# New engine orders and engine choices for a windowed-attention and channel-mix kernel, planned with another rule for the shared port

## The chip, the core and the metric

The kernel runs on one core of a Trainium2 chip. A core has five engines with a queue of instructions each: TensorE (PE in the profile, with PEld for its weight loads), VectorE (DVE), ScalarE (ACT), GpSimd (POOL) and SyncE (SP), which here only starts DMAs. Each engine takes its own queue strictly in order, and engines wait for one another through semaphores. The metric is the device time of one execution in microseconds, lower is better.

## The reference

Attention over a causal window of 128 keys plus four sink keys, for 4 batches, 8 heads, 768 positions and 64 dimensions a head; then a channel mix over the 512 columns that the eight heads make together.

```python
scores = scale * np.matmul(q, k.transpose(0, 1, 3, 2))
is_sink = pos[None, :] < int(n_sink)                       # n_sink = 4
in_window = (rel >= 0) & (rel < int(window))               # rel = query - key, window = 128
scores = np.where(is_sink | in_window, scores, -1000000000.0)
a = np.exp(scores - max); a = a / (sum(a) + 1e-09)
x = np.matmul(a, v)                                        # then (B, S, 512)
x_prev = x shifted by one position
xk = mu_k * x + (1.0 - mu_k) * x_prev
xr = mu_r * x + (1.0 - mu_r) * x_prev
k = np.maximum(xk @ w_k, 0.0)                              # 512 -> 1024
out = 1.0 / (1.0 + np.exp(-(xr @ w_r))) * (k * k @ w_v)
```

## The kernel before

The positions are cut into twelve units of 256, three for each batch. A unit goes through these steps.

- **Load** (SP; L462 to L486, weights L505): q, k and v in 32-bit into three buffers each (`qs`, `ks`, `vs`). The weights come through three more (`w`).
- **Cast** to bf16 (L689, L693 or L698 for q and k into `qb` and `kb`, half a unit at a time; L770 for v into `vb`; L650 to L656 for the weights). Each may stand on ScalarE, VectorE or GpSimd; w_v is not cast by GpSimd.
- **Transpose** of q and k, on TensorE (L733, L738) with a copy out of PSUM (L751, L756, on ScalarE or VectorE), or by a transposing DMA for the units in `KD` and `QD`, 5 and later (L715).
- **Attend**: scores for two pairs of heads (L845), exponentials on ScalarE (L917), multiplication with the mask on VectorE (L931, tile `e`), sinks (L814, L821, then L888 or L903, the full or the tiled form of the same product), values (L950), reciprocal (L964) and scaling (L967, tile `x`) on VectorE.
- **Mix**: `x` is transposed to `xt` (L991 with a copy at L1000, or a DMA, L1011), a difference `td` (L1027) and from it `xk` and `xr` (L1040), all on VectorE but the copy.
- **FFN**: `xk` times w_k (L1117), relu (L1127 on ScalarE or L1131 on VectorE, tile `rl`), square (L1139, VectorE), `xr` times w_r (L1148), tanh (L1154), the square times w_v (L1166), the gate's product `ob` (L1175, VectorE), and the store (L1182). The last 128 rows have their own form (L1087, L1097).

No loop sets the order of the work. The program first lists 1028 operations, numbered as they are listed. Each has an engine, a price, the data it reads and writes, and the buffers that it takes and holds. The table `CHOICE` gives the engine or the form of the operations that could stand in several. The table `ORDER` gives, for each engine, the list of its operations in the order in which it takes them. `Plan.schedule` walks the five lists together by the prices; since each list is fixed, what it settles is which free buffer an operation gets, how the engines' parts are interleaved as the program is written, and where early fillers go: matmuls on the tile `warm` (L1226, L1229, L1232) whose results nobody reads, put where the plan sees TensorE idle before 28.5 us.

The plan takes VectorE and GpSimd to share a port to the on-chip memory, and marks operations that need it with `port=True`: casts, products of two tiles of that memory and stores started by GpSimd, but not operations that read PSUM, such as `x`, reciprocals, relus and `ob`. While one engine holds the port the plan lets no marked operation of the other begin.

```python
if o["port"]:
    t = max(t, port.get("DVE" if engine == "POOL" else "POOL", 0.0))
```

The program itself holds nothing of this rule: no semaphore stands for the port.

Of the kernel before, what the change touches and what calls it, by code (L numbers as in the profile page):

```python
# [18 lines left out]
    80: "ACT", 81: "POOL", 82: "ACT", 83: "POOL", 84: "POOL", 85: "ACT", 86: "ACT",  # L19
    88: "ACT", 90: "DVE", 96: "POOL", 98: "DVE", 99: "DVE", 101: "DVE", 102: "ACT",  # L20
    103: "ACT", 129: "POOL", 132: "DVE", 135: "POOL", 141: "ACT", 144: "DVE", 151:
    "DVE", 160: "PE/full", 172: "PE/full", 183: "POOL", 186: "DVE", 189: "POOL",
    192: "POOL", 195: "ACT", 196: "DVE", 198: "DVE", 242: "PE/full", 265: "DVE",
    268: "DVE", 271: "POOL", 273: "DVE", 274: "POOL", 277: "DVE", 278: "ACT", 352:
    "POOL", 355: "POOL", 361: "DVE", 380: "DVE", 428: "POOL", 432: "POOL", 438:
    "ACT", 496: "PE/full", 511: "POOL", 516: "ACT", 517: "ACT", 587: "POOL", 591:
    "ACT", 592: "ACT", 628: "POOL", 661: "POOL", 663: "POOL", 665: "ACT", 666:
    "ACT", 675: "DVE", 736: "POOL", 741: "ACT", 785: "POOL", 810: "POOL", 815:
    "DVE", 855: "POOL", 888: "DVE", 889: "ACT", 929: "POOL", 945: "PE/full", 998:
    "DVE", 1002: "DVE", 1006: "DVE", 1010: "DVE", 1019: "POOL",  # L30
# [17 lines left out]
FETCH = (17500.0, 28500.0, 36900.0, 47800.0, 57300.0, 66500.0, 78000.0, 85500.0,  # L48
         96000.0, 104000.0, 113000.0, 126000.0, 135000.0, 147000.0, 161000.0)
# [45 lines left out]
    ),  # L95
    "DVE": (
# [25 lines left out]
    ),  # L122
    "ACT": (
# [1166 lines left out]
```

## Time and profile before

| | |
|---|---|
| median of three runs | 166.36 us (165.06, 166.36, 167.31) |
| span of the profiled execution | 163.8 us; the profile gives no other time for it |
| from the span to the median | 2.5 us |
| chain that ended last, by engine | PE 69%, DVE 11%, DMA 10%, SP's queue 5% |
| DMA | 24.12 MB read, 6.29 MB written |
| GpSimd waiting for `ob` before a store | 47.0 us in 5 waits |

The span runs from the first to the last instruction of one execution; the runs' times hold what lies around it too. A group of instructions is written as line, engine, operation, tiles out<-in, shapes, count, then busy us and the mean ns of one, then the idle time ahead of it and who ended it. VectorE's and ScalarE's instructions overlap a little: one starts before the one ahead of it has ended, so sums of durations are above the busy time.

### The profile page before, as it was taken

How to read it: one execution, taken by the hardware profiler on the slowest of the kernel's cores; microseconds unless marked ns; L12 is line 12 of the kernel's file. 1: busy time of each engine (PE TensorE's matmuls, PEld its weight loads, DVE VectorE, ACT ScalarE, POOL GpSimd, SP SyncE). 2: the span in 40 equal slices, each digit the busy share in tenths (PEclk: the TensorE clock that was granted, in tenths of full speed). 3: DMA queues.
4: the chain of work that ended last, by engine and by line, in shares of the span. 5: the costliest groups of instructions: out<-in, count | busy, mean ns of one | idle time of the engine just before them, and what ended most of it. 6: DMA issues, size and time to landing. Idle time of an engine off the chain costs nothing.

```text
span 163.8 us, 4680 instructions
## 1 busy us (share of the span) xinstructions
PE 154.4 (94%) x1845; PEld 100.8 (62%) x1845; DVE 148.4 (91%) x383; ACT 121.4 (74%) x198; POOL 32.7 (20%) x61
## 2 busy tenths in 40 slices
PE   7989779899999999999999999999999999999991
PEld 2446458675468558777656666855385756578450
DVE  2589999999999999999999999998898989999931
ACT  3779899999999998999996689882499694152020
POOL 6643543222731022111103001032000100101001
PEclk9999999999999999999999999999999999999998
DMA  4999999999999999999997998979999963251032
GB/s 138 250 334 275 400 346 205 362 397 338 200 289 238 265 233 225 196 179 189 276 233 174 254 196 218 242 188 119 239 162 201 268 79 98 57 203 64 0 144 112
DMA packets 78821, 35.16 MB, mean 215 GB/s; under 512 B 68744, under 2 KB 71056, under 8 KB 78800
## 3 DMA queue, kind: packets, MB, share of 16 engines
q1 hardware_dynamic: 78384, 33.56, 85.8%
q0 software_dynamic: 400, 1.31, 2.3%
q8 instruction: 14, 0.23, 0.6%
q14 instruction: 7, 0.06, 0.1%
q10 hardware_dynamic: 16, 0.00, 0.0%
HBM read 24.12 MB, written 6.29 MB: 186 GB/s over the span
## 4 chain that ended last, share of the span: by engine, by line
PE 69%; DVE 11%; DMA 10%; SPq 5%; issue 2%; ACT 1%; POOL 0%; DVEq 0%; POOLq 0%
PE bank L1117 22%; PE bank L1166 19%; PE bank L1148 9%; PE bank L950 6%; DMA ks<-in_k_dram 5%; PE sc L845 4%; DMA kt<-kb 4%; DVE e L931 3%; SPq L462 3%; PE bank L1232 3%; DVE xk L1040 2%; DVE x L967 2%; PE bank L903 1%; SPq L479 1%; PE bank L991 1%
## 5 line engine op out<-in xcount | busy, mean ns | idle before, releaser
L1117 PE MATMUL bank<-xk,wk_sb 128*128 128x256 bf16 x384 | 47.3, 273 | 0.7 <-ACT rl L1127 0.5
L917 ACT ACTIVATE e<-sc 128x1024 bf16<-128x1024 f32 (+1 forms) x48 | 44.4, 966 | 3.4 <-PE sc L845 3.3
L1166 PE MATMUL bank<-wv_h,kk 128*128 128x512 bf16 x184 | 44.9, 379 | 0.0
L1117 PEld LDWEIGHTS <-wk_sb 128*128 128x128 bf16 x384 | 36.2, 98 | 7.0 <-issue 0.9
L931 DVE TENSOR_TENSOR e<-e,mask 128x1024 bf16<-128x1024 bf16 (+1 forms) x48 | 31.7, 676 | 0.0
L1127 ACT ACTIVATE rl<-bank 128x512 bf16<-128x512 f32 x43 | 25.1, 606 | 8.1 <-PE bank L1117 7.9
L1154 ACT ACTIVATE th<-bank 128x512 f32<-128x512 f32 x24 | 14.3, 608 | 18.2 <-PE bank L1148 11.4
L1166 PEld LDWEIGHTS <-kk 128*128 128x128 bf16 x184 | 17.0, 98 | 16.4
L1148 PE MATMUL bank<-wr_sb,xr 128*128 128x512 bf16 x96 | 23.8, 379 | 0.0
L1040 DVE SCALAR_TENSOR_TENSOR xk<-td,mu_all,xt 128x256 bf16<-128x256 bf16 x48 | 23.2, 511 | 0.0
L1040 DVE SCALAR_TENSOR_TENSOR xr<-td,mu_all,xt 128x256 bf16<-128x256 bf16 x48 | 22.4, 477 | 0.0
L967 DVE TENSOR_TENSOR x<-bank,rec 128x256 bf16<-128x256 f32 x48 | 19.5, 418 | 0.5
L1139 DVE TENSOR_TENSOR kk<-rl 128x512 bf16<-128x512 bf16 x48 | 19.3, 416 | 0.3 <-ACT rl L1127 0.2
L1175 DVE SCALAR_TENSOR_TENSOR ob<-th,bank 128x512 f32<-128x512 f32 x23 | 15.6, 682 | 2.4 <-PE bank L1166 1.1
L950 PE MATMUL bank<-vb,e 128*128 128x65 bf16 x352 | 16.5, 194 | 0.3
L950 PEld LDWEIGHTS <-e 128*128 128x128 bf16 x352 | 13.8, 97 | 3.5 <-DVE e L931 0.7
L1148 PEld LDWEIGHTS <-xr 128*128 128x128 bf16 x96 | 9.0, 98 | 9.6
L845 PE MATMUL sc<-qt,kt 64*64 64x128 bf16 (+3 forms) x496 | 12.6, 226 | 0.4 <-DMA kt<-kb 0.3
L1182 POOL DMA_DIRECT2D out_dram<-ob x5 | 2.8, 570 | 47.0 <-DVE ob L1175 47.0
L845 PEld LDWEIGHTS <-kt 64*64 64x64 bf16 (+1 forms) x496 | 9.0, 106 | 4.1 <-issue 1.4
L1027 DVE TENSOR_TENSOR td<-xt 128x512 bf16<-128x512 bf16 x24 | 10.1, 433 | 0.1
L770 ACT CAST vb<-vs 128x512 bf16<-128x512 f32 x14 | 8.8, 636 | 0.2 <-DMA vs<-in_v_dram 0.2
(93 smaller groups left out, 157.7 us busy)
## 6 DMA issues: line engine op xcount, KB each, us to landing
vs<-in_v_dram SPq DMA_DIRECT2D x24, 256.0 KB, 5.5
out_dram<-ob SPq DMA_DIRECT2D x18, 256.0 KB, 3.4
ks<-in_k_dram SPq DMA_DIRECT2D x16, 256.0 KB, 4.6
qs<-in_q_dram SPq DMA_DIRECT2D x12, 256.0 KB, 4.7
qs<-in_q_dram SPq DMA_DIRECT2D x6, 512.0 KB, 7.5
ks<-in_k_dram SPq DMA_DIRECT2D x4, 512.0 KB, 9.6
w<-in_moe_w_k_dram SPq DMA_DIRECT2D x2, 1024.0 KB, 8.8
w<-in_moe_w_v_dram SPq DMA_DIRECT2D x2, 1024.0 KB, 11.3
```

The source lines that it names most:

```text
L845: nc.tensor.matmul(out=sc[keys, a, o0 + f0 - q0:o0 + f1 - q0], lhsT=lhs[rows, keys], rhs=qs[rows, f0:f1], start=u not in BIAS, stop=True, ...
L917: nc.scalar.activation(out=buf[ek][:, :, lo:], in_=buf[sck][:, :, lo:], func=AF.Exp, scale=scale)
L931: nc.vector.tensor_tensor(out=at, in0=at, in1=m, op=ALU.mult)
L950: nc.tensor.matmul(out=o[:, g, a, :], lhsT=e[:, a, e0:e0 + 128], rhs=rhs, start=(T == 0 and i == 0), stop=(i == len(blocks) - 1), skip_gro ...
L967: P.op("DVE", dve(256), lambda ok=ok, rk=rk, c=c: nc.vector.tensor_tensor(out=buf["x", u][:, :, 128 * c:128 * c + 128].rearrange("p g (a d ...
L1040: nc.vector.scalar_tensor_tensor(out=buf[key][:, c, :], in0=buf[tk][:, i, :], scalar=mu[w][:, c:c + 1], in1=xt[:, c, t0 - 1:t0 + 255], op0 ...
L1117: nc.tensor.matmul(out=ps[:, i, :], lhsT=wk_sb[:, c, 128 * f:128 * f + 128], rhs=xk[:, c, :], start=(c == 0), stop=(c == NC - 1), skip_gro ...
L1127: nc.scalar.activation(out=buf[rk], in_=buf[psk].rearrange("p (i t) -> p i t", i=2), func=AF.Relu)
L1139: P.op("DVE", dve(512, 0.52), lambda f2=f2, rk=rk: nc.vector.tensor_tensor(out=buf["kk", u][:, 2 * f2:2 * f2 + 2, :], in0=buf[rk], in1=buf ...
L1148: nc.tensor.matmul(out=buf[psk], lhsT=buf["xr", u][:, c, 128 * g:128 * g + 128], rhs=wr_sb[:, c, :], start=(c == 0), stop=(c == NC - 1))
L1166: nc.tensor.matmul(out=buf[psk], rhs=wv_h[:, f, :], lhsT=buf["kk", u][:, f, 128 * g:128 * g + 128], start=(f == 0), stop=(f == NF - 1))
L1175: P.op("DVE", dve(512), lambda psk=psk, tk=tk, bk=bk: nc.vector.scalar_tensor_tensor(out=buf[bk], in0=buf[tk], scalar=1.0, in1=buf[psk], o ...
```

## The change

One line of the rule changes. A cast on GpSimd now holds the port in the plan for its price less 165 ns, where it was 0.58 of its price; `FETCH`, the moments at which the plan expects a fetch of instructions to delay the DMAs, has other numbers; and both tables were made anew, `ORDER` for all five engines and `CHOICE` with more entries.

```diff
-    80: "ACT", 81: "POOL", 82: "ACT", 83: "POOL", 84: "POOL", 85: "ACT", 86: "ACT",
+    80: "DVE", 81: "POOL", 82: "POOL", 83: "ACT", 84: "ACT", 85: "POOL", 86: "ACT",
...
-FETCH = (17500.0, 28500.0, 36900.0, 47800.0, 57300.0, 66500.0, 78000.0, 85500.0,
-         96000.0, 104000.0, 113000.0, 126000.0, 135000.0, 147000.0, 161000.0)
+FETCH = (17200.0, 24600.0, 35000.0, 47000.0, 53500.0, 62300.0, 71300.0, 80800.0, 90700.0,
+         102000.0, 111300.0, 123300.0, 132500.0, 145000.0)
...
     "DVE": (
-        70, 90, 71, 99, 98, 101, 109, 114, 111, 112, 106, 79, 116, 117, 132, 125,
+        70, 71, 93, 90, 95, 96, 98, 132, 114, 109, 129, 134, 131, 125, 106, 120,
...
             if o["port"]:
-                port[o["engine"]] = t + (0.58 * cost if o["engine"] == "POOL" else cost)
+                port[o["engine"]] = t + (max(0.0, cost - 165.0) if o["engine"] == "POOL" else cost)
```

No operation is added or removed; only the fillers go from 16 to 19. What stands on another engine than before:

- Early casts (q and k of units 0 to 4, v of units 0 to 3, and the weights): GpSimd makes 16 instead of 14, three of them weights before and after. Later casts: 22 instead of 13.
- VectorE, units 0 to 4: it gives up six casts of q, k and v, three copies of `xt` and two copies of `qt` or `kt` out of PSUM; it takes three casts, four copies of `qt` or `kt`, two relus and a quarter of w_k.
- In all: ScalarE eight operations fewer, VectorE three fewer, GpSimd eleven casts more and five stores fewer, SP five stores more.

Of the pairs of sink products the full form goes from 5 to 4, the tiled one from 11 to 12.

In the changed file all lines of the kernel's body stand 21 further down (L719 is L698). In the rows below the number in a tile's name tells its buffers apart; the number after the underscore has no meaning.

**VectorE at the start.** Before, from its fifth instruction on:

```order
L557 MEMSET hmask_150 128x520
L698 CAST kb0_79<-ks0_67 128x4x2x64
L561 MEMSET ksink0_151 128x64
L561 MEMSET ksink1_152 128x64
L561 MEMSET vsink0_153 128x520
L561 MEMSET vsink1_154 128x520
```

Now, from the last two of the same memsets on:

```order
L588 MEMSET sc0_61 64x2x64
L588 MEMSET sc1_62 64x2x64
L719 CAST qb0_82<-qs0_70 128x4x2x64
L719 CAST kb0_79<-ks0_67 128x4x2x64
L777 COPY qt0_89<-bank0_63 128x512
L719 CAST kb0_79<-ks0_67 128x4x2x64
L777 COPY kt0_85<-bank3_66 128x512
L710 CAST qb1_83<-qs1_71 128x2x4x64
L952 TENSOR_TENSOR e0_93<-e0_93,mask0_147 128x2x384
L952 TENSOR_TENSOR e1_94<-e1_94,mask0_147 128x2x384
L710 CAST kb1_80<-ks1_68 128x2x4x64
L772 COPY qt1_90<-bank3_66 128x128x4
```

All twelve memsets stand ahead of the first cast, three casts of unit 0 follow, and the cast of unit 1's q stands ahead of the first masks.

**SP at the start.** The first loads before:

```order
L486 DMA ks0_67<-in_k_dram 128x4x128
L486 DMA qs0_70<-in_q_dram 128x4x128 x2
L486 DMA ks0_67<-in_k_dram 128x4x128
L462 DMA vs0_73<-in_v_dram 128x8x64 x2
L479 DMA ks1_68<-in_k_dram 128x2x512
L479 DMA qs1_71<-in_q_dram 128x2x512
```

and now:

```order
L507 DMA qs0_70<-in_q_dram 128x4x128
L507 DMA ks0_67<-in_k_dram 128x4x128
L507 DMA qs0_70<-in_q_dram 128x4x128
L507 DMA ks0_67<-in_k_dram 128x4x128
L500 DMA qs1_71<-in_q_dram 128x2x512
L500 DMA ks1_68<-in_k_dram 128x2x512
L483 DMA vs0_73<-in_v_dram 128x8x64 x2
```

q comes ahead of k, and unit 1's q and k have moved ahead of unit 0's v.

**GpSimd's early casts.** Before, after the constants:

```order
L698 CAST kb0_79<-ks0_67 128x4x2x64
L621 COPY vsink0_153<-hmask_150 128x8
L621 COPY vsink1_154<-hmask_150 128x8
L787 COPY ksink0_151<-kt0_85 64x4x4 x2
L689 CAST kb1_80<-ks1_68 128x2x4x64 x2
L689 CAST qb2_84<-qs2_72 128x2x4x64
L770 CAST vb1_136<-vs1_74 128x8x64
L689 CAST kb2_81<-ks2_69 128x2x4x64 x2
L656 CAST wk_sb_139<-w320_76 128x4x256
L656 CAST wk_sb_139<-w321_77 128x4x256
```

and now:

```order
L719 CAST qb0_82<-qs0_70 128x4x2x64
L594 AFFINE_SELECT mask_146<-ones_157 128x128 x2
L710 CAST kb1_80<-ks1_68 128x2x4x64
L791 CAST vb0_135<-vs0_73 128x8x64
L808 COPY ksink0_151<-kt0_85 64x4x4 x2
L710 CAST kb2_81<-ks2_69 128x2x4x64 x2
L710 CAST qb2_84<-qs2_72 128x2x4x64
L791 CAST vb1_136<-vs1_74 128x8x64
L710 CAST qb2_84<-qs2_72 128x2x4x64
L710 CAST kb0_79<-ks0_67 128x2x4x64
L677 CAST wk_sb_139<-w320_76 128x4x256
L791 CAST vb2_137<-vs2_75 128x8x64
```

GpSimd now casts v of units 0, 1 and 2 and both halves of q of unit 2; the first weight stands behind nine short casts where it stood behind seven, and one half of k of unit 1 is no longer here.

More of the change, by code (lines that the diff above doesn't have):

```diff
@@ L18 @@
 CHOICE = {
-    80: "ACT", 81: "POOL", 82: "ACT", 83: "POOL", 84: "POOL", 85: "ACT", 86: "ACT",
[L20 to L30, printed above, removed]
+    80: "DVE", 81: "POOL", 82: "POOL", 83: "ACT", 84: "ACT", 85: "POOL", 86: "ACT",
@@ new lines @@
+    87: "DVE", 88: "ACT", 89: "DVE", 90: "DVE", 92: "ACT", 93: "DVE", 95: "DVE", 96:
+    "DVE", 98: "DVE", 99: "POOL", 101: "ACT", 102: "POOL", 103: "ACT", 129: "DVE",
+    131: "DVE", 132: "DVE", 134: "DVE", 135: "POOL", 137: "ACT", 138: "ACT", 140:
+    "ACT", 141: "POOL", 142: "ACT", 144: "ACT", 151: "ACT", 160: "PE/tiles", 172:
+    "PE/full", 183: "POOL", 185: "ACT", 186: "POOL", 188: "ACT", 189: "POOL", 191:
+    "ACT", 192: "POOL", 194: "ACT", 195: "ACT", 196: "POOL", 198: "ACT", 205: "ACT",
@@ new lines @@
+    213: "ACT", 217: "DVE", 221: "ACT", 225: "ACT", 234: "SP", 238: "SP", 242:
+    "PE/full", 254: "PE/tiles", 265: "POOL", 267: "ACT", 268: "ACT", 270: "ACT",
+    271: "ACT", 273: "ACT", 274: "ACT", 276: "ACT", 277: "POOL", 278: "POOL", 283:
+    "ACT", 290: "ACT", 298: "ACT", 302: "DVE", 306: "ACT", 310: "ACT", 319: "SP",
+    323: "SP", 346: "POOL", 348: "DVE", 349: "ACT", 351: "ACT", 352: "ACT", 354:
+    "ACT", 355: "ACT", 357: "ACT", 358: "POOL", 359: "POOL", 361: "DVE", 368: "ACT",
+    376: "ACT", 380: "ACT", 384: "ACT", 388: "ACT", 397: "SP", 401: "SP", 405:
@@ new lines @@
+    "PE/tiles", 417: "PE/tiles", 428: "POOL", 429: "POOL", 431: "ACT", 432: "POOL",
+    434: "ACT", 436: "ACT", 437: "POOL", 438: "DVE", 440: "ACT", 447: "ACT", 455:
+    "ACT", 459: "ACT", 463: "ACT", 467: "ACT", 476: "SP", 480: "SP", 484:
+    "PE/tiles", 496: "PE/tiles", 507: "POOL", 508: "POOL", 510: "ACT", 511: "ACT",
+    513: "POOL", 515: "ACT", 516: "ACT", 517: "POOL", 522: "ACT", 529: "ACT", 537:
+    "ACT", 541: "ACT", 545: "ACT", 549: "ACT", 558: "SP", 562: "SP", 585: "ACT",
+    586: "ACT", 587: "ACT", 589: "ACT", 591: "POOL", 592: "ACT", 607: "ACT", 611:
@@ new lines @@
+    "ACT", 615: "ACT", 619: "ACT", 628: "SP", 632: "SP", 636: "PE/tiles", 648:
+    "PE/tiles", 659: "ACT", 660: "ACT", 661: "POOL", 663: "POOL", 665: "ACT", 666:
+    "ACT", 668: "ACT", 675: "ACT", 683: "ACT", 687: "ACT", 691: "ACT", 695: "ACT",
+    704: "SP", 708: "SP", 712: "PE/tiles", 724: "PE/tiles", 735: "ACT", 736: "POOL",
+    737: "ACT", 739: "POOL", 741: "POOL", 742: "POOL", 760: "ACT", 764: "ACT", 768:
+    "ACT", 772: "ACT", 781: "SP", 785: "SP", 808: "POOL", 809: "ACT", 810: "ACT",
@@ L31 @@
+    812: "DVE", 814: "POOL", 815: "ACT", 830: "ACT", 834: "ACT", 838: "ACT", 842:
+    "ACT", 851: "SP", 855: "SP", 859: "PE/tiles", 871: "PE/tiles", 882: "ACT", 883:
+    "POOL", 884: "ACT", 886: "DVE", 888: "POOL", 889: "POOL", 904: "ACT", 908:
+    "ACT", 912: "ACT", 916: "ACT", 925: "SP", 929: "SP", 933: "PE/full", 945:
+    "PE/full", 970: "ACT", 974: "ACT", 978: "ACT", 982: "ACT", 991: "SP", 995: "SP",
+    998: "DVE", 1002: "ACT", 1006: "DVE", 1010: "DVE", 1019: "SP",
 }
```

138 rows, old and new, of the table ORDER are left out of this document.

## Prediction

> **What bounds the kernel now.** I read the page's busy shares first, then the busy time by stage, then the waits at the start, then VectorE's groups of instructions early against late. The first two lines come from the page, the others from the view by stage (stretch in us; length, then for each engine its busy us and instructions; granted clock; DMA share; GB/s).
>
> ```profile
> span 163.8 us, 4680 instructions
> PE 154.4 (94%) x1845; PEld 100.8 (62%) x1845; DVE 148.4 (91%) x383; ACT 121.4 (74%) x198; POOL 32.7 (20%) x61
> ...
> core 0: us, PE busy (x) PEld busy (x) DVE busy (x) ACT busy (x) POOL busy (x), PEclk, DMA share, GB/s
> ...
> 10.00:45.00 35.00, 31.06 (x433) 20.94 (x434) 34.74 (x85) 32.81 (x52) 14.13 (x16) 1.00 1.05 321
> 45.00:110.00 65.00, 64.90 (x887) 45.04 (x887) 63.84 (x169) 58.44 (x100) 9.12 (x15) 1.00 1.03 225
> 110.00:145.00 35.00, 34.69 (x391) 21.64 (x390) 32.64 (x86) 20.23 (x32) 2.45 (x6) 1.00 0.85 159
> ```
>
> From 10 to 45 us VectorE is busy 34.74 of 35 us and TensorE only 31.06: VectorE sets the pace. From 45 us TensorE is busy 64.90 of 65 and then 34.69 of 35: it sets the pace, and VectorE is 1.16 and 2.36 us below full, 3.5 us together. The granted clock is 1.00 throughout. So the end is the moment at which enough matmul work stands ready, plus a fixed line of matmuls: a microsecond that VectorE gains before 45 us comes off the end, one that it gains later does not, and one that it loses later costs nothing until the 3.5 us are used up. The chain that ended last says the same (start, us, what): VectorE's operations early, matmuls late, with a piece between them that runs over a load.
>
> ```profile
> 12.42 0.42 DVE x L967
> ...
> 28.00 0.41 DVE xk L1040
> 28.52 1.87 SPq L479
> ...
> 35.36 8.95 DMA ks<-in_k_dram
> 44.43 0.62 POOL kb L693
> ...
> 142.92 3.49 PE bank L1117 x32
> ```
>
> **The sum.** It has four terms and is made on the span, 163.8 us. The three runs shown have a median of 166.36 us, 2.5 us above it; I carry a change of the span to the median one for one.
>
> *Term 1, the port.* The rows that bear on it, first VectorE's groups from 10 to 46 us, then the same groups from 46 us on (xcount | busy us, mean ns):
>
> ```profile
> L931 DVE TENSOR_TENSOR e<-e,mask 128x1024 bf16<-128x1024 bf16 x8 | 6.7, 857 | 0.0
> L1040 DVE SCALAR_TENSOR_TENSOR xk<-td,mu_all,xt 128x256 bf16<-128x256 bf16 x9 | 5.5, 625 | 0.0
> L967 DVE TENSOR_TENSOR x<-bank,rec 128x256 bf16<-128x256 f32 x12 | 4.8, 412 | 0.1
> ...
> L931 DVE TENSOR_TENSOR e<-e,mask 128x768 bf16<-128x768 bf16 x7 | 4.1, 608 | 0.0
> L1027 DVE TENSOR_TENSOR td<-xt 128x512 bf16<-128x512 bf16 x6 | 2.8, 470 | 0.0
> L689 DVE CAST qb<-qs 128x512 bf16<-128x512 f32 x3 | 1.7, 555 | 0.0
> ...
> L1040 DVE SCALAR_TENSOR_TENSOR xk<-td,mu_all,xt 128x256 bf16<-128x256 bf16 x39 | 17.7, 485 | 0.0
> L931 DVE TENSOR_TENSOR e<-e,mask 128x1024 bf16<-128x1024 bf16 x24 | 16.2, 684 | 0.0
> L1027 DVE TENSOR_TENSOR td<-xt 128x512 bf16<-128x512 bf16 x18 | 7.3, 421 | 0.1
> L931 DVE TENSOR_TENSOR e<-e,mask 128x768 bf16<-128x768 bf16 x9 | 4.8, 546 | 0.0
> ```
>
> The same instruction is longer early: 8 x (857-684) + 9 x (625-485) + 7 x (608-546) + 6 x (470-421) ns is 1.38 + 1.26 + 0.43 + 0.29, and the three casts, 0.14 us each above the 0.41 of the undisturbed one quoted below, add 0.4: **3.8 us** of VectorE's time. Where it goes is seen when one operation is laid beside GpSimd's cast (timelines: start, us):
>
> ```profile
> 15.94 0.62 POOL L770 CAST vb<-vs 128x512 bf16<-128x512 f32 x1 [1.02 <-DMA vs<-in_v_dram]
> 16.00 0.83 DVE L1040 SCALAR_TENSOR_TENSOR xk<-td,mu_all,xt 128x256 bf16<-128x256 bf16 x1
> 21.51 1.51 POOL L656 CAST wk_sb<-w 128x1024 bf16<-128x1024 f32 x1 [1.87 <-DMA w<-in_moe_w_k_dram]
> 22.05 1.52 DVE L931 TENSOR_TENSOR e<-e,mask 128x1024 bf16<-128x1024 bf16 x1
> 40.11 1.89 POOL L689 CAST qb<-qs 128x512 bf16<-128x512 f32 x1 [6.39 <-DMA qs<-in_q_dram]
> ```
>
> The xk of 16.00 ends at 16.83; less the 0.485 that it takes undisturbed it was let go at 16.35, and the cast ended at 16.56. The e of 22.05 ends at 23.57, so it was let go at 22.89; the cast ended at 23.02. The hold ends 0.13 to 0.21 us before the cast does, as the new table has it (0.165). The old table ended it after 0.58 of its price: for a cast priced 620 ns after 360 instead of 455, for one priced 1100 after 638 instead of 935. Of the early casts (q and k of units 0 to 4, v of units 0 to 3 and the weights) GpSimd makes 11 of the short and 3 of the long kind, so 11 x 0.095 + 3 x 0.297 = 1.9 us of hold lay where the old order believed the port free, half of the 3.8. The change gives GpSimd 13 short and 3 long casts there; two more, at 0.095 each as the least, take 0.2 back. I take **-1.7 us**. The ends: all 3.8 us go, or nothing does and two more casts at 3.8/14 = 0.27 us each add 0.5.
>
> The Trainium skill, "SBUF — State Buffer", section "Who interferes with whom", says that whichever of the two engines issues first keeps the shared ports for the whole instruction. This trace shows 0.13 to 0.21 us less than that; by the page the old table left the whole 3.8 us uncounted (11 x 0.26 + 3 x 0.46 is more than that) and the new one leaves 16 x 0.165 = 2.6, the term would be 2.6 - 3.8 = -1.2 and the sum 165.2.
>
> *Term 2, work that changes engines in units 0 to 4.* VectorE gives up six casts, three xt copies and two copies out of PSUM, and takes three casts, four copies out of PSUM, two relus and one w_k cast. Prices, from the timeline at the start and the groups over the whole run:
>
> ```profile
> 6.22 0.41 DVE L698 CAST qb<-qs 128x512 bf16<-128x512 f32 x1
> 8.57 0.69 DVE L756 COPY kt<-bank 128x512 bf16<-128x512 bf16 x1 [1.95 <-PE bank L738]
> 9.18 0.68 DVE L756 COPY qt<-bank 128x512 bf16<-128x512 bf16 x1
> ...
> L1131 DVE TENSOR_SCALAR rl<-bank 128x512 bf16<-128x512 f32 x5 | 3.3, 685 | 0.3 <-PE bank L1117 0.3
> L1000 DVE COPY xt<-bank 128x512 bf16<-128x512 bf16 x5 | 2.1, 413 | 0.0
> L654 DVE TENSOR_SCALAR wv_h<-w 128x1024 bf16<-128x1024 f32 x2 | 1.4, 684 | 0.0
> ```
>
> The copy of 9.18 starts 0.08 before the one of 8.57 ends, so an operation costs 0.08 less than its row: a cast 0.33, an xt copy 0.33, a copy out of PSUM 0.61, a relu or (by the nearest row, L654) a w_k cast 0.60. Given up: 6 x 0.33 + 3 x 0.33 + 2 x 0.61 = 4.2. Taken: 3 x 0.33 + 4 x 0.61 + 2 x 0.60 + 0.60 = 5.2. That is **+1.0 us**. The ends: 0, where ScalarE, busy 32.81 of the 35 us, was what VectorE's order really followed, and +2.5, where what is given up would have come after 45 us anyway.
>
> *Term 3, the first waits.*
>
> ```profile
> 3.82 0.56 DVE L698 CAST kb<-ks 128x512 bf16<-128x512 f32 x1 [1.98 <-DMA ks<-in_k_dram]
> 4.58 1.04 DVE L561 MEMSET vsink<- 128x520 bf16 x2
> 4.69 0.62 ACT L698 CAST qb<-qs 128x512 bf16<-128x512 f32 x1 [2.38 <-DMA qs<-in_q_dram]
> 7.47 0.61 POOL L698 CAST kb<-ks 128x512 bf16<-128x512 f32 x1 [1.52 <-DMA ks<-in_k_dram]
> ```
>
> VectorE waits 1.98 us for the first load and 1.95 at 8.57: 3.9 in all. Its memsets run from 4.34 to 6.29; the change puts them ahead of the first cast, into the first wait, where their 1.9 us just fit. VectorE is then there at 3.82 and takes a cast that ScalarE had. But the loads still land at 3.82, 4.69 and 7.47, and VectorE's third cast is now the one that waits for 7.47: I count 0.1 + 0.3 + 1.7 and, for the transposes ahead of its next copy, 0.6, or 2.7 us of waits instead of 3.9. The q and k of unit 1 are now fetched ahead of unit 0's v, and the cast of that q stands ahead of VectorE's first masks; I allow 0.2 for it. **-1.0 us**. The ends: -1.95, the memsets' whole time, and 0, all of it lost to the later loads.
>
> *Term 4, the rest, at nothing.* ScalarE loses eight instructions; it is not the bound after 45 us. GpSimd has nine more of the later casts (22 for 13): VectorE's 3.5 us below full cover them, and without that cover each costs up to 0.455 (second rival). Five stores go from GpSimd's queue to SP's, where the loads behind them wait until ob is made; three buffers of each input cover that, and uncovered a load is late by one such wait. The last store was SP's already. On TensorE one pair of sink products changes from four full matmuls to eight on quarters of the array, and three fillers are added where it waits anyway; without that wait the first would cost 8/88 of 3.5 us, 0.3, less the full ones' own, and a filler its 0.4 us:
>
> ```profile
> L903 PE MATMUL bank<-vsink,es 64*64 64x130 bf16 x88 | 3.5, 226 | 0.0
> ...
> L1229 PE MATMUL bank<-warm 128*128 128x512 bf16 x6 | 2.5, 422 | 0.0
> ```
>
> -1.7 + 1.0 - 1.0 = -1.7 us: span 162.1, median **164.7 us**.
>
> **The rivals.**
>
> First: *the stall goes nearly whole, and the memsets' time with it.* For it: VectorE has x operations, which read PSUM and are not lengthened early (412 ns, no more than an undisturbed cast's 0.41 us), to lay beside a cast. -3.8 + 1.0 - 1.95 = -4.8: 161.6 us. Against it: casts start when their loads land, which no order fixes.
>
> Second, on the other side: *GpSimd's late casts become VectorE's new bound.* There are 22 of them instead of 13, on a VectorE with 3.5 us to spare. At a hold of 0.455 each, all stalling, 22 x 0.455 - 3.5 = +6.5 us: 171.2. At the early price, 22 x 0.27 - 3.5 = +2.4: 167.1. It decides for slower by 2% from 0.39 us a cast, (169.7 - 164.7 + 3.5)/22. Against it: the 13 late ones of now leave e at 684 ns. The Trainium skill, "Perfetto Trace Analysis", section "Optimizing Scalar/DVE Operations", warns that moving work between these two engines may not help since they share a port; the early rows bear it out, the late ones do not yet.
>
> Third: *nothing of the port is won.* The order is fixed while loads land when they land, so casts meet VectorE's operations as often as before, or the piece of the chain from 28.5 to 44.4 us, over SP's queue and a load of 8.95 us, takes back what VectorE gains. +0.5 + 1.0 - 1.0 = +0.5: 166.9 us. The new rule in the code alone moves nothing, since the lists set the order.
>
> **How the numbers follow.** Two per cent, about what a measurement of this kernel can tell from no change, is 3.3 us: faster is below 163.0, slower above 169.7. The forecast, 163.2 to 166.0, has 0.43; the first rival 0.20, the second 0.12, of which 0.08 lies above 169.7; the third 0.25. Of the forecast 0.04 falls below 163.0. So faster 0.24, same 0.68, slower 0.08. The range runs from near the first rival's 161.6 to past the third's 166.9 and the second's 167.1: 161.8 to 167.6, about 0.18 left out.
>
> **What would show it.** Right: VectorE's e (1024) and xk of the first 45 us fall from 857 and 625 ns to about 770 and 550; its waits before 10 us sum to some 2.9 us; TensorE is full from about 43 us. Wrong: early e above 820 ns; late e well above 684 (second rival); TensorE waiting after 45 us for a GpSimd cast (40.11 shows one of 1.89 us where 0.61 is its own length) or a load behind a store on SP.

## The result: 170.6 us, slower by 2.65%

| | before | after |
|---|---|---|
| median of 6 runs | 166.62 us (165.06 to 167.31) | 170.62 us (170.15 to 171.6) |
| ratio | | 1.0265, 95% interval 1.021 to 1.0321 |
| span of the profiled execution | 163.8 us | 169.9 us (its time 171.6) |

The profiled execution of the changed kernel is the longest of its six; their spans go from 168.4 to 169.9 us. So the two profiles differ by 6.1 us where the medians differ by 4.0, and a difference of 1 us between two profiles proves nothing here. The ratio, 1.0265, makes the loss 4.4 us of 166.4; the sections below reckon with ratios.

First the page of the changed kernel (busy us and share of the span, then the chain that ended last by engine), then the view by stage with the columns of before:

```profile
span 169.9 us, 4681 instructions
PE 155.0 (91%) x1834; PEld 100.5 (59%) x1853; DVE 152.3 (90%) x380; ACT 118.0 (69%) x190; POOL 36.6 (22%) x67
...
PE 41%; DVE 34%; DMA 16%; issue 3%; SPq 3%; ACT 1%; DVEq 0%; ACTq 0%
```

```profile
10.00:45.00 35.00, 30.12 (x435) 20.43 (x435) 34.12 (x80) 32.13 (x52) 13.61 (x19) 1.00 1.03 314
45.00:110.00 65.00, 62.69 (x852) 42.01 (x861) 63.55 (x160) 55.33 (x91) 13.85 (x22) 1.00 1.08 205
110.00:145.00 35.00, 33.65 (x383) 21.43 (x386) 32.48 (x85) 20.64 (x33) 3.46 (x5) 1.00 0.89 177
```

TensorE's busy time is 0.6 us longer than before (155.0 and 154.4); the rest of the 6.1 us is time in which it has nothing to do. It was full after 45 us and is no longer: 62.69 of 65 us and 33.65 of 35, where it had 64.90 and 34.69. VectorE's share of the chain went from 11% to 34%. The granted clock is 1.00 in all three stretches, as before.

The same by coarser stages, before and then after (the same columns); length less TensorE's busy time is its idle time:

```profile
0.00:45.00 45.00, 39.56 (x470) 24.88 (x471) 39.70 (x105) 38.80 (x61) 20.02 (x40) 1.00 0.99 295
45.00:60.00 15.00, 14.90 (x217) 10.21 (x217) 14.73 (x40) 14.27 (x25) 2.65 (x5) 1.00 1.15 258
60.00:145.00 85.00, 84.69 (x1061) 56.48 (x1059) 81.75 (x215) 64.39 (x107) 8.92 (x15) 1.00 0.93 192
```

```profile
0.00:45.00 45.00, 37.44 (x469) 24.08 (x471) 39.59 (x101) 36.19 (x58) 19.29 (x41) 1.00 0.97 296
45.00:60.00 15.00, 13.58 (x177) 8.78 (x180) 14.62 (x34) 13.17 (x22) 4.67 (x6) 1.00 0.80 169
60.00:145.00 85.00, 82.76 (x1071) 54.66 (x1072) 81.40 (x211) 62.80 (x102) 12.63 (x20) 1.00 1.05 199
```

TensorE's idle time grows from 5.44 to 7.56 us up to 45 us (+2.12), from 0.10 to 1.42 up to 60 us (+1.32) and from 0.31 to 2.24 up to 145 us (+1.93). With the 0.6 us of busy time this is 5.97 of the 6.1.

VectorE's groups of 10 to 46 us, the first five of the changed kernel and the last two of the kernel before, for two groups that the prediction did not show (xcount, busy us, mean ns):

```profile
L1061 DVE SCALAR_TENSOR_TENSOR xk<-td,mu_all,xt 128x256 bf16<-128x256 bf16 x12 | 7.0, 600 | 0.0
L952 DVE TENSOR_TENSOR e<-e,mask 128x1024 bf16<-128x1024 bf16 x8 | 6.3, 791 | 0.0
L1061 DVE SCALAR_TENSOR_TENSOR xr<-td,mu_all,xt 128x256 bf16<-128x256 bf16 x9 | 5.1, 572 | 0.0
...
L1048 DVE TENSOR_TENSOR td<-xt 128x512 bf16<-128x512 bf16 x6 | 3.3, 542 | 0.5 <-ACT xt L1021 0.5
...
L675 DVE TENSOR_SCALAR wv_h<-w 128x1024 bf16<-128x1024 f32 x2 | 1.8, 895 | 0.0
```

```profile
L1040 DVE SCALAR_TENSOR_TENSOR xr<-td,mu_all,xt 128x256 bf16<-128x256 bf16 x9 | 4.3, 473 | 0.0
...
L654 DVE TENSOR_SCALAR wv_h<-w 128x1024 bf16<-128x1024 f32 x2 | 1.4, 684 | 0.0
```

The mean of e fell from 857 to 791 ns and that of xk from 625 to 600. But xr rose from 473 to 572, td from 470 to 542, and the two casts of w_v from 684 to 895. Above the late rows that the prediction used: 8 x (791-684) + 12 x (600-485) + 6 x (542-421) ns is 0.86 + 1.38 + 0.73; xr and w_v above their undisturbed rows of before are 9 x 0.099 + 2 x 0.211 = 0.89 + 0.42. Together 4.3 us, where the prediction's sum was 3.8: the stall did not shrink, it changed its victims. Counted instruction by instruction, each against the usual length of its form, VectorE is lengthened by 4.3 us in twelve places before 50 us and 0.26 after 60 us in the old profile, and by 5.4 us in fourteen places before 50 us and 2.6 in nine after 60 us in the new one. This excess is called the lengthening below. The early part does not hang on one profile: with the old lists of the start and all casts in place it is 3.8 to 4.7 us before 50 us in three profiles (before, e1, e11; e1 to e18 are the runs of the experiments below), with the new ones 4.3 to 6.2 us in eleven (after, e6 to e10, e13 to e16, e18).

One of these, VectorE's and GpSimd's timelines at the same place (start, us):

```profile
30.59 1.51 DVE L952 TENSOR_TENSOR e<-e,mask 128x1024 bf16<-128x1024 bf16 x1
...
30.52 1.04 POOL L677 CAST wk_sb<-w 128x1024 bf16<-128x1024 f32 x1 [1.19 <-DMA w<-in_moe_w_k_dram]
```

GpSimd had waited 1.19 us for the weight; the cast began when the load landed, 0.07 us ahead of e, and e took 1.51 us instead of 0.69. It ends at 32.10, so it was let go at 31.41, 0.15 us before the cast's end at 31.56. The list does not set when that load lands.

The start, VectorE's timeline:

```profile
3.79 0.60 DVE L719 CAST qb<-qs 128x512 bf16<-128x512 f32 x1
4.64 0.43 DVE L719 CAST kb<-ks 128x512 bf16<-128x512 f32 x1 [0.25 <-DMA ks<-in_k_dram]
5.44 0.69 DVE L777 COPY qt<-bank 128x512 bf16<-128x512 bf16 x1 [0.38 <-PE bank L759]
8.27 0.43 DVE L719 CAST kb<-ks 128x512 bf16<-128x512 f32 x1 [2.14 <-DMA ks<-in_k_dram]
9.19 0.69 DVE L777 COPY kt<-bank 128x512 bf16<-128x512 bf16 x1 [0.49 <-PE bank L759]
10.05 0.43 DVE L710 CAST qb<-qs 128x512 bf16<-128x512 f32 x1 [0.17 <-DMA qs<-in_q_dram]
```

The waits sum to 3.4 us instead of 3.9. The fourth load let its cast begin at 8.27 us, where it was 7.47. That is this profile and not the order. In twelve of the thirteen other profiles with the same first loads (e3, e5 to e10, e13 to e18) the fourth load landed between 7.0 and 7.6 us, and in the thirteenth at 8.6. The same cast in the kernels e6 and e16:

```profile
7.31 0.43 DVE L718 CAST kb<-ks 128x512 bf16<-128x512 f32 x1 [1.40 <-DMA ks<-in_k_dram]
7.05 0.43 DVE L711 CAST kb<-ks 128x512 bf16<-128x512 f32 x1 [0.21 <-DMA ks<-in_k_dram]
```

VectorE's idle time up to 20 us is 5.4 us in the profile of the changed kernel. In the eleven others with the new start and its casts in place (e5 to e10, e13 to e16, e18) it is 3.9 to 5.4 us, and 6.2 in e10, whose granted clock was 0.83 from 10 to 20 us; the middle one has 4.4. With the old start it is 5.2 us in three profiles (before, e4, e11) and 5.9 in e1.

### The profile page after: what moved, and what is told of

It is laid out like the page before. It is cut to its first block, busy times and chain, and to the rows that moved or that the text cites. A ratio compares the mean times of both kernels' runs of the same rounds, so it can differ in the third digit from the quotient of the medians.

```text
span 169.9 us, 4681 instructions
## 1 busy us (share of the span) xinstructions
PE 155.0 (91%) x1834; PEld 100.5 (59%) x1853; DVE 152.3 (90%) x380; ACT 118.0 (69%) x190; POOL 36.6 (22%) x67
## 4 chain that ended last, share of the span: by engine, by line
PE 41%; DVE 34%; DMA 16%; issue 3%; SPq 3%; ACT 1%; DVEq 0%; ACTq 0%
PE bank L1187 12%; PE bank L1138 12%; DMA kt<-kb 8%; DVE e L952 6%; PE bank L1169 6%; DVE xr L1061 5%; DVE xk L1061 5%; DMA ks<-in_k_dram 5%; DVE kk L1160 4%; PE bank L971 4%; DVE x L988 4%; DMA out_dram<-ob 3%; PE sc L866 3%; DVE td L1048 3%; DVE ob L1196 2%
## 5 line engine op out<-in xcount | busy, mean ns | idle before, releaser
L1138 PE MATMUL bank<-xk,wk_sb 128*128 128x256 bf16 x384 | 50.1, 273 | 1.5 <-DVE ob L1196 1.3
L1187 PE MATMUL bank<-wv_h,kk 128*128 128x512 bf16 x176 | 43.9, 379 | 0.9 <-DVE wv_h L675 0.3
L1138 PEld LDWEIGHTS <-wk_sb 128*128 128x128 bf16 x384 | 35.3, 98 | 8.8 <-issue 2.0
L1148 ACT ACTIVATE rl<-bank 128x512 bf16<-128x512 f32 x43 | 26.0, 605 | 11.6 <-PE bank L1138 10.3
L1061 DVE SCALAR_TENSOR_TENSOR xr<-td,mu_all,xt 128x256 bf16<-128x256 bf16 x48 | 24.5, 516 | 0.0
L1061 DVE SCALAR_TENSOR_TENSOR xk<-td,mu_all,xt 128x256 bf16<-128x256 bf16 x48 | 24.2, 523 | 0.1
L791 POOL CAST vb<-vs 128x512 bf16<-128x512 f32 x15 | 11.3, 758 | 59.6 <-DMA vs<-in_v_dram 47.0
L1160 DVE TENSOR_TENSOR kk<-rl 128x512 bf16<-128x512 bf16 x48 | 20.4, 438 | 0.5 <-ACT rl L1148 0.4
L1048 DVE TENSOR_TENSOR td<-xt 128x512 bf16<-128x512 bf16 x24 | 10.8, 458 | 0.5 <-ACT xt L1021 0.5
L1021 ACT COPY xt<-bank 128x512 bf16<-128x512 bf16 x13 | 7.5, 590 | 3.5 <-PE bank L1012 3.3
```

Source lines behind the costliest of these rows:

```text
L1061: nc.vector.scalar_tensor_tensor(out=buf[key][:, c, :], in0=buf[tk][:, i, :], scalar=mu[w][:, c:c + 1], in1=xt[:, c, t0 - 1:t0 + 255], op0 ...
L1138: nc.tensor.matmul(out=ps[:, i, :], lhsT=wk_sb[:, c, 128 * f:128 * f + 128], rhs=xk[:, c, :], start=(c == 0), stop=(c == NC - 1), skip_gro ...
L1148: nc.scalar.activation(out=buf[rk], in_=buf[psk].rearrange("p (i t) -> p i t", i=2), func=AF.Relu)
L1160: P.op("DVE", dve(512, 0.52), lambda f2=f2, rk=rk: nc.vector.tensor_tensor(out=buf["kk", u][:, 2 * f2:2 * f2 + 2, :], in0=buf[rk], in1=buf ...
L1187: nc.tensor.matmul(out=buf[psk], rhs=wv_h[:, f, :], lhsT=buf["kk", u][:, f, 128 * g:128 * g + 128], start=(f == 0), stop=(f == NF - 1))
```

## The experiments

The expectations speak of a *lag*. Each weight load on TensorE gets a fixed price by its line (109 ns in L1117, 216 in L1148 and L1166, and so on); their running sum is the matmul work done, a little over 140 us in all. The lag at work 60 is the moment at which the sum reaches 60, less that moment in the profile of before (76.9 us). It comes from single profiles and is good to about 1 us. The ratios are against runs of the kernel before on the same chip.

### The rule, the port and the order apart

**The new rule with the old tables.** The old `CHOICE` and `ORDER` in the changed file.

```diff
     "DVE": (
-        70, 71, 93, 90, 95, 96, 98, 132, 114, 109, 129, 134, 131, 125, 106, 120,
+        70, 90, 71, 99, 98, 101, 109, 114, 111, 112, 106, 79, 116, 117, 132, 125,
...
```

> The old lists and engine choices with the new port rule and the new FETCH. Theory (all of the loss lies in the lists and choices): 166.6 us, within 0.8 of the kernel before. Rival (the rule or FETCH moves buffers or fillers so that something waits): above 168.

166.44 us, ratio 1.0013 (0.9977 to 1.0049). The rule alone moves nothing; what changed the time is in the two tables.

**The port taken away, in the old order and in the new one.**

```diff
+    def tiny_copy(out, in_):
+        nc.gpsimd.memset(out, 0.0)
+        nc.gpsimd.tensor_copy(out=out[..., 0:1], in_=in_[..., 0:1])
...
-                           "POOL": (620.0, cast(nc.gpsimd.tensor_copy), True)},
+                           "POOL": (620.0, cast(tiny_copy), True)},
```

> The old kernel with each GpSimd cast of q, k, v and weights replaced by a memset of the target and a cast of one column, so that the load is still waited for but hardly anything is read: the numbers come out wrong by that. Port theory: the 4.6 us by which VectorE's instructions are lengthened now, 4.3 of them before 50 us, mostly go: 162 to 163.5 us. Rival (the lengthening lies beside other waits): 165.5 or more.

> The same replacement in the new kernel, which lengthens VectorE's instructions by 8.0 us. Port theory, all of the loss: the new order without stalls is no slower than the old one without them, 162 to 164 us. Order theory (the new order makes VectorE do more ahead of the matmuls, apart from the port): it stays 2 us or more above the old kernel with small casts, 165 us or more.

Old order: 163.34 us, 0.9828 (0.976 to 0.9897), with 0.6 us of lengthening left. New order: 166.39 us, 0.9992 (0.9952 to 1.0031), with 1.0 us left. In ratios, the port costs the old order 0.0172 and the new one 1.0265 - 0.9992 = 0.0273; without it the new order is still 0.9992 - 0.9828 = 0.0164 behind. In us of 166.4 that is 2.9, 4.5 and 2.7. So the loss of 4.4 us has two parts: **the port costs 1.7 us more than before, and the order itself 2.7 us**. With the intervals of the ratios put together as a root of squares, an estimate, that is 1.7 us give or take 1.6 and 2.7 give or take 1.3. That the port became cheaper by the forecast 1.7 us is ruled out; that it became dearer is only just clear of nothing by the times, and the early lengthening above says the same.

The edit has one more effect: where a whole cast of 512 columns takes 0.61 us, the cast of one column takes 0.22, so its reader could start earlier. It hardly did: up to 50 us TensorE's weight loads wait for GpSimd's casts for 1.6 us instead of 1.8 in the old order and for 0.6 as before in the new one.

**GpSimd's early casts, and its late ones.** The same edit for one half of the casts at a time (for v and, in the first kernel, the weights likewise):

```diff
+                           "POOL": (620.0, cast(tiny_copy if u <= 5 else nc.gpsimd.tensor_copy), True)},
```

> The changed kernel with GpSimd's casts of q and k of units 0 to 5, of v of units 0 to 3 and of the weights (19, up to 47.5 us) replaced by a memset and a cast of one column in each row piece, so that these inputs are wrong; the 19 later ones are as they were. Theory (the loss is early: VectorE's 5.4 us of lengthening before 50 us pass on nearly whole, since the new start leaves VectorE no slack): the lag at matmul work 30 falls from 3.5 us to about -1, and the time by 3.2 to 4 us to about 167. Rival (late casts matter as much): it falls by about 2 us, to 168.6.

> The changed kernel with only the 19 later casts of GpSimd (q and k of units 6 to 11, v of units 4 to 11) replaced in that way. Theory (late casts cost little): the time falls by at most 0.8 us, to 169.8 or more, and TensorE's waits from 60 to 145 us stay at 1.2 us or more. Rival (the 2.6 us by which VectorE is lengthened after 60 us hold TensorE up): it falls by about 2 us, to 168.6.

Early casts small: 166.86 us, 1.002 (0.9985 to 1.0055). Late casts small: 170.18 us, 1.0232 (1.0179 to 1.0285). The 19 casts up to 47.5 us cost 1.0265 - 1.002 = 0.0245, 4.1 us; the 19 later ones 1.0265 - 1.0232 = 0.0033, 0.5 us, which the intervals do not tell from nothing, though VectorE has no lengthening left after 50 us in that profile. By stage, with the early casts small:

```profile
0.00:45.00 45.00, 40.62 (x488) 26.42 (x490) 39.34 (x108) 38.41 (x63) 21.41 (x60) 1.00 1.00 301
45.00:60.00 15.00, 14.41 (x248) 9.97 (x249) 14.74 (x37) 13.93 (x23) 4.25 (x9) 1.00 1.00 215
```

TensorE's idle time up to 60 us falls from 8.98 to 4.97 us. That this is as much as the time is partly luck: in the ten other profiles with the new start, the new lists up to 60 us and all early casts in place (e6 to e10, e13 to e16, e18) it lies between 6.5 and 9.1 us. The second expectation's other number failed: TensorE's idle time from 60 to 145 us fell to 1.14 us, just below the 1.2, and the median did not follow.

**Start and rest apart.** The first 300 operations in one order, the rest in the other.

```diff
+first = one_order[:300]
+rest = [i for i in other_order if i not in first]
+ORDER = {e: [i for i in first + rest if engine[i] == e] for e in ENGINES}
```

> The first 300 operations (to about 45 us) in the old order and on the old engines, the others in the new order and on the new engines. Matmul work stood done 3.4 us later at 50 us and 6.0 us later at 125 us in the new kernel's profile. Theory (the start carries over half): 1.5 to 2.5 us above the old kernel, 168.1 to 169.1. Rival (the rest carries no loss, late casts are covered): 166.6 to 167.2.

> The first 300 operations in the new order and on the new engines, the others as in the old kernel. Theory (the start carries over half): 2.5 to 3.5 us above the old kernel, 169.1 to 170.1. Rival (what the start loses is made up later by idle time of VectorE): 166.6 to 168.

Old start with new rest: 169.66 us, 1.0205 (1.0158 to 1.0251). New start with old rest: 170.35 us, 1.0258 (1.0204 to 1.0312). Both are above what was expected of them. Together that is 0.0463, more than the whole change, so the cut itself costs: TensorE is idle for 2.23 and 2.34 us from 45 to 60 us. They do not divide the loss; the pair above, which cuts nothing, does. What they add is the shape: with the old rest the lag stays as it is from 57 us on (3.8 at work 40, 3.6 at work 135), with the new rest it grows by 2.1 us from work 60 on even behind the old start.

### What holds TensorE up after 60 us

In the changed kernel's profile the lag grows from 3.1 at work 60 to 6.2 at the end; without the port it grows from -2.0 to 0.7. So the order's own 2.7 us seem to be lost late. Nine kernels looked for the cause, and one more made the same edit in the kernel before.

**Stores, late casts, a store ahead of loads.**

```diff
-    628: "SP", 785: "SP", 855: "SP",
+    628: "POOL", 785: "POOL", 855: "POOL",
...
-    507: "POOL", 508: "POOL", 513: "POOL",
+    507: "ACT", 508: "ACT", 513: "ACT",
...
     "SP": (
-        238, 25, 34, 26,
+        25, 34, 26, 238,
```

> The new kernel with the five stores back in GpSimd's queue. Theory of SP's queue: in the new profile VectorE's ob at 126.4 and 130.2 us waits 1.2 us for a store that stands behind transposes and loads in SP's queue, and matmuls behind it; without that 1.0 to 1.5 us less, 169.1 to 169.6. Rival (the late loss is the port's): no change, 170.2 to 171.

> The new kernel with eleven casts of units 6 to 11 moved from GpSimd to ScalarE, each in ScalarE's list where it ran in the new profile. Port theory for the late part: VectorE's instructions are lengthened by 2.6 us from 60 us on, against 0.3 in the old kernel; that falls to under 0.8 and the time by 1 to 2 us, 168.6 to 169.6. Rival (VectorE's spare time covers it, or ScalarE is late instead): 170.2 or more.

> The new kernel with one store of unit 0 moved behind three loads (both halves of v of unit 4 and q of unit 6) in SP's queue, as in the old order. In the new profile SP waits for that store's ob until 49.8 us and the loads run dry (29 GB/s from 47 to 51 us). Theory of SP's queue: the hole closes and 0.5 to 1.5 us go, 169.1 to 170.1. Rival (VectorE is the bound there, the loads are early enough): no change, 170.3 to 171.

> The three edits together: stores back with GpSimd, eleven late casts with ScalarE, the store behind the loads. If the late loss is these three it is 2.5 to 3.5 us less than the new kernel, 167.1 to 168.1, and the rest above the old kernel is the start. If the late loss is the order of the other lists: above 169.5.

The five stores back on GpSimd: 170.98 us, 1.0296 (1.0212 to 1.038). Eleven late casts on ScalarE: 170.38 us, 1.0249 (1.0198 to 1.0301). One store put behind three loads on SP: 170.12 us, 1.0241 (1.0176 to 1.0307). All three: 170.39 us, 1.024 (1.0183 to 1.0296). No interval stands apart from that of the changed kernel. The second of them speaks against the rival of the late casts, although its lengthening after 60 us fell only to 1.6 us and not below the expected 0.8; the late half of the port pair, where none is left, says the same. The third undid a wait that the chain of the changed kernel shows (start, us, what), with SP's queue held by a store until 49.8 us and two loads and a transpose behind it:

```profile
50.18 1.95 DMA vs<-in_v_dram
52.13 7.56 DMA kt<-kb
```

**Less work for VectorE from unit 6 to 9.**

```diff
+                if 6 <= u <= 9:
+                    at, m = at[:, 0:at.shape[1] // 2], m[:, 0:m.shape[1] // 2]
                 nc.vector.tensor_tensor(out=at, in0=at, in1=m, op=ALU.mult)
```

> The changed kernel with half of the multiplication with the mask left out in units 6 to 9: sixteen VectorE operations of about 0.68 or 0.55 us fall to about 0.42 or 0.34, some 3.8 us of VectorE's work in the stretch in which TensorE goes from 60 to 110 us of its matmul work. Theory (in that stretch the new lists ask VectorE for 47.4 us of work where the old ones ask for 45.6, so VectorE sets the pace there and TensorE waits for it): the lag behind the kernel before no longer grows from work 60 to 135 (it grew by 3.1 us), and the time falls by 2.5 to 3.5 us to about 167.5. Rival (the late loss is made by TensorE's own order, by ScalarE or by stores): the growth stays at 2 us or more and the time is above 169.5.

> The same half of the mask left out in units 6 to 9 of the kernel before. Theory: with the old lists TensorE sets the pace there, with 0.6 us of real waits after 60 us, so the time falls by no more than 0.8 us, to 165.8 or more. Rival (VectorE sets the pace in both orders alike): it falls by 2.5 us or more, as far as in the changed kernel.

The changed kernel: 170.82 us, 1.0299 (1.0241 to 1.0357). The kernel before: 165.76 us, 0.9995 (0.9955 to 1.0034). The theory that VectorE sets the pace late in the new order fell: 3.8 us less of its work gained nothing in either, and the lag still grows by 2.7 us.

**The waits around 130 us.** In the changed kernel ScalarE waits for the last unit's loads of k ahead of two relus, VectorE's gate product for a store, and TensorE for both (timelines of ScalarE, VectorE and TensorE):

```profile
125.59 0.62 ACT L714 CAST kb<-ks 128x512 bf16<-128x512 f32 x1 [1.30 <-DMA ks<-in_k_dram]
128.31 0.62 ACT L714 CAST kb<-ks 128x512 bf16<-128x512 f32 x1 [1.61 <-DMA ks<-in_k_dram]
...
130.23 0.69 DVE L1196 SCALAR_TENSOR_TENSOR ob<-th,bank 128x512 f32<-128x512 f32 x1 [1.07 <-DMA out_dram<-ob]
...
129.48 1.02 PE L1169 MATMUL bank<-wr_sb,xr 128*128 128x512 bf16 x3 [0.26 <-ACT rl L1148]
130.97 0.60 PE L1138 MATMUL bank<-xk,wk_sb 128*128 128x256 bf16 x4 [0.46 <-DVE ob L1196]
```

```diff
-    882: "ACT", 883: "POOL", 884: "ACT",
+    882: "POOL", 883: "POOL", 884: "POOL",
...
-    pool("ob", 3, [128, Dm], FP32)
+    pool("ob", 4, [128, Dm], FP32)
```

> The changed kernel with the two casts of the last unit's k on GpSimd instead of ScalarE, where they waited 1.30 and 1.61 us for their loads at 125.6 and 128.3 us with relus queued behind them. Theory (an instruction that waits for a load holds up the relu behind it on ScalarE, and TensorE waits for the relu): those relus come 1 to 1.5 us earlier, TensorE's idle time from 120 to 145 us falls from 1.27 us to 0.7 or less, and the time falls by 0.4 to 0.9 us against the changed kernel's 170.6. Rival (something else sets the pace there, such as the gate product's wait for a store): idle time and time stay as they are.

> The changed kernel with four buffers for the gate's product ob instead of three: VectorE no longer waits at 126.35 and 130.23 us (0.15 and 1.07 us) for a store to free one. Theory (that wait holds up VectorE's xk and with it TensorE's wait of 0.46 us at 130.97): TensorE's idle time from 120 to 145 us falls from 1.27 us to about 0.8 and the time by 0.3 to 0.6 us, to about 170.2. Rival: no change.

> Both of these. Theory: TensorE's idle time from 120 to 145 us falls to 0.3 us or less and the time by about 1 us, to 169.4 to 169.8; more than 1.5 us is not in it, since the lag behind the kernel before at 115 us is 5.2 of 6.2 us. Rival: no change, or the waits move to other operations.

171.25 us, 1.0306 (1.0255 to 1.0357); 170.74 us, 1.0254 (1.0203 to 1.0305); 170.95 us, 1.0284 (1.0241 to 1.0327). The waits that were aimed at went; the stretch of 120 to 145 us, of the first kernel, of the second, of the one with both edits, and of the one with a store behind three loads (e8), whose edit lies far ahead, at 49.8 us:

```profile
120.00:145.00 25.00, 24.68 (x311) 15.99 (x314) 24.28 (x63) 15.27 (x23) 3.02 (x4) 1.00 0.71 159
```

```profile
120.00:145.00 25.00, 24.79 (x316) 16.49 (x317) 24.46 (x63) 16.27 (x25) 1.91 (x2) 1.00 0.70 154
```

```profile
120.00:145.00 25.00, 22.98 (x301) 15.17 (x303) 22.71 (x58) 14.88 (x22) 2.91 (x4) 1.00 0.85 174
```

```profile
120.00:145.00 25.00, 25.00 (x316) 16.10 (x315) 24.35 (x62) 15.76 (x24) 1.30 (x2) 1.00 0.75 160
```

TensorE's idle time there is 0.32 and 0.21 us instead of 1.27, but 2.02 with both edits, where 0.3 or less was expected (in an execution longer than that kernel's median), and none at all in e8. The medians did not fall. So the 1.27 us were in good part the mark of one profile rather than of every execution.

**New lists to 105 us, old ones from there.**

```diff
+first = new_order[:650]
+rest = [i for i in old_order if i not in first]
+ORDER = {e: [i for i in first + rest if engine[i] == e] for e in ENGINES}
```

> New lists for the first 650 operations in the order of the program (to about 105 us), the old lists for the rest. If the late loss lies behind 105 us alone: the lag at matmul work 85 is about 4.4 us as in the changed kernel and stays there, TensorE's idle time from 120 us on is 0.4 us or less, and the time is 168.5 to 169.5. If it lies ahead of 105 us or is spread: the time is 170 or more. Differences at the cut can add up to 1 us of a wait there, to be seen in the trace.

170.2 us, 1.0235 (1.0189 to 1.0282), by its own mark "ahead of 105 us or spread". In the profile the lag is 4.8 at work 85 and 4.4 at work 135; a wait of 0.63 us stands at the cut. That gives back 0.5 us, give or take 1.2, so the lists behind 105 us are most likely a small part of the loss.

### A way to make the port cheaper

**Each cast on GpSimd in two halves, in the kernel before.**

```diff
+    def half_copy(out, in_):
+        n = out.shape[1] // 2
+        nc.gpsimd.tensor_copy(out=out[:, 0:n], in_=in_[:, 0:n])
+        nc.gpsimd.tensor_copy(out=out[:, n:], in_=in_[:, n:])
```

> The kernel before with every cast on GpSimd made as two instructions of half the width, nothing else moved. Theory (a VectorE operation that meets a cast waits until 0.13 to 0.21 us before that instruction's end, so a shorter instruction means a shorter wait): VectorE's lengthening falls from 4.6 us to about 2.5 and the time by 0.5 to 2 us, to about 165. Rival (GpSimd takes the port again for its second half before VectorE does): the lengthening stays at 4 us or more, the casts take longer, and the time is 166.3 or more.

165.29 us, 0.9955 (0.9915 to 0.9995): a gain of 0.7 us, just clear of nothing. But the lengthening as a whole did not fall as the theory had it. In the profiled execution, which at 167.7 us is the longest of its ten, it is 4.78 us in 27 places where it was 4.57 in 13: a meeting costs 0.18 us instead of 0.35, and there are twice as many. Where it lies did change: before 50 us it is 3.2 us, where the three profiles with the old lists have 3.8 to 4.7, and after 60 us 1.6 instead of 0.26. Since late lengthening cost little above, that would account for the gain; with one profile it is not shown. It is the only version that leaves nothing out and came out below the kernel before.

## Why the prediction was wrong

It forecast 164.7 us in a range of 161.8 to 167.6 and gave 0.08 to slower by 2%.

- **Term 1, the port (-1.7): nothing of it was won back.** The step that failed is "half of the 3.8 lay where the old order believed the port free", taken as time that an order can win back. The rows give 4.3 us instead of 3.8 before 46 us, and the port's cost rose by 1.7 us, give or take 1.6 (small casts in both orders). The pessimistic end, +0.5, is inside that interval; the forecast -1.7 is not. The reason against it stood in the text, under the first and third rivals: casts start when loads land. The cast at 30.52 us is one such meeting, and the fourth load, which landed between 7.0 and 8.6 us in profiles of the same loads, shows that a load moves by more than the tenths of a us by which the plan keeps operations apart. How many of the meetings come about in this way was not counted.
- **The hold itself was read rightly.** The e of 30.59 us was let go 0.15 us before the cast's end, within the 0.13 to 0.21 that were read off. With the casts made small the lengthening went nearly whole (0.6 and 1.0 us left). That the rule in the code moves nothing was right too (1.0013).
- **Terms 2, 3 and 4 (+1.0 - 1.0 + 0 = 0) came to +2.7**, give or take 1.3, the order's loss without the port; this is the larger miss. Of term 3 the waits fell by 0.5 us in the profile of the changed kernel, not by 1.2, and VectorE then idles 0.84 us from 10 to 20 us where it idled 0.19. But that profile has a late fourth load. By the idle time up to 20 us in the other profiles, 4.4 us in the middle instead of 5.2, some 0.8 of the forecast 1.0 was had, as an estimate. So the 2.7 us have to be looked for in term 2 and in term 4, which stood at nothing. The lag without the port, -2.0 at work 60 and 0.7 at the end, points at term 4, whose work lies late, and not at term 2; these two were not measured apart. Of term 4 the covers held for the stores (1.0296 with them back) and for the late casts (1.0249 without eleven of them).
- **"A fixed line of matmuls" after 45 us did not hold** for the new order: TensorE's idle time from 45 to 145 us went from 0.41 to 3.66 us. Other profiles bring the two closer: with the old lists it is 2.15 us in e1, with the new ones 2.4 to 4.5 us in e6 to e10, e13 to e15 and e18. Part of it is early loss arriving late, since the early casts alone bring 45 to 60 us down from 1.42 to 0.59.
- **The rivals.** The first (the stall goes nearly whole, 161.6) fell with term 1. The second (late casts bind VectorE) would have given 167.1 to 171.2 and so held the time, but for the wrong reason: two kernels speak against it. The third (nothing of the port is won, 166.9) had the port's part right and was 3.7 us too low, since it took over terms 2 to 4.
- **The signs to watch** were partly ill chosen: e (1024) at 791 and xk at 600 ns looked like half a success while xr, td and w_v took the stalls over. The sum over all of VectorE's forms would have been the sign.

What stays open is where the order's own 2.7 us lie. Taking away VectorE's load, the late casts, the stores, the waits around 130 us or the lists behind 105 us gave back 0.6 us at the most, so none of them is likely to be the main part. The intervals of these differences reach 1.2 to 1.7 us to each side, so none is strictly excluded either. That several engines wait by turns, a little everywhere, is what the traces look like; it was not shown.

## What to carry to other kernels

In this kernel a plan did not keep two engines off a shared port where one of them starts on a load. Where that is so, count the meetings as a cost and not as something that a better list removes: 0.35 us each here, and spread over GpSimd's 17 casts before 50 us in the old order 4.3/17 = 0.25 us a cast, not far below the 0.33 us for which VectorE makes the cast itself. Before a new order is priced, it pays to measure the ceiling: the kernel with the contention taken away told that 2.9 us were to be had at all, and that the new order was 2.7 us worse without any contention. And a wait that one profile shows need not be in the median: waits of about 1 us were removed here three times without a gain, and a load that came late in one profile was early in nearly all the others. A second profile of the same lists is the cheaper test.

## What the hardware showed that was not expected

- A memset on GpSimd does not do what a cast does. With each cast replaced by a memset of the same tile and a cast of one column, GpSimd was as busy as ever (40.1 us in the span, 36.6 with the casts) and VectorE's lengthening fell from 8.0 to 1.0 us.
- Halving a cast halves the wait of the operation that meets it, 0.35 to 0.18 us, and doubles the number of meetings, 13 to 27, in the one profile taken.
- A wait at the port is not paid in full: 4.57 us of lengthening cost the old order 2.9 us, 8.0 the new one 4.5. Of the latter, 5.4 early ones cost 4.1 and some 2.6 late ones about 0.5; the intervals of these prices reach 1.1 to 1.3 us to each side.
